# One level of Strassen's algorithm for the product of h and w2, in groups of 256 tokens

## The chip, the cores and the metric

The kernel runs on one core of a Trainium2 chip. The metric is the device time of one execution in microseconds (us). Times are medians of several executions; only executions in the fast state are compared. One slow execution occurred in the study and is named where it occurred. Engines are named as in the profile: PE is TensorE, PEld its weight loads, DVE VectorE, ACT ScalarE, POOL GpSimd. A record is one matmul in the trace; each fp32 matmul of the program leaves two. The pitch is the distance from the start of one record to the start of the next. The banks are those of PSUM, the memory into which TensorE writes; a bank is emptied (evicted) when ScalarE or VectorE has read it out. "Kernel before" and "changed kernel" are the two that the prediction compares.

## The reference

The program is an attention block with a threshold, followed by a Fourier mixing block and a channel MLP. All data are fp32.

```python
# attention: q, k, v of shape (8, 8, 576, 64)
scores = scale * np.matmul(q, k.transpose(0, 1, 3, 2))
thresh = np.max(scores, axis=-1, keepdims=True) - tau
scores = np.where(scores >= thresh, scores, -1000000000.0)
attn = softmax(scores)                       # written out in the reference
x = (attn @ v).transpose(0, 2, 1, 3).reshape(8, 576, 512)
# mixing
mixed = np.real(np.fft.fft(np.fft.fft(x, axis=1), axis=2))
u = x + mixed
un = (u - mean(u)) / np.sqrt(var(u) + 1e-06)
ch = np.maximum(un @ w_ch1, 0.0) @ w_ch2     # w_ch1 512 x 2048, w_ch2 2048 x 512
return u + ch                                # 4608 rows (tokens) of 512
```

Only the last product, `h @ w_ch2`, changes its algorithm. It has 4608 x 2048 x 512 multiplications and is one of the two largest.

## The kernel before

Eight sequences are taken in turn; each has four pairs of heads, and each pair is worked off in five steps of 128 query rows. A step computes scores, does the softmax on ScalarE and VectorE, and transposes the weights of the step before through PSUM. Between these parts `fill()` puts pieces of the mixing and of the MLP of earlier sequences into the stream of TensorE:

```python
for i in range(2 * per_batch, total + 1):
    if i < total:
        scores(i)
        softmax(i)
    fill()
    n, t = divmod(i, NT)
    transposed_weights(i - 1)      # pe, pw, pw: three PSUM banks, emptied by ScalarE
    if t == 3 and n + 1 < B * NPAIR:
        prep_pair(n + 1)           # pq, pk, pt: three more banks
    fill()
    fill()
    ...                            # weighted values, folding, start of a batch
```

The MLP works on groups of 384 tokens. `u_t` holds u transposed in a ring of two sequences. All PSUM tiles of this code except the scores share four banks (`tag="mm", bufs=4`):

```python
def channels(g):                                  # GT = 384, NJ = 16, ND = 4, DM = 512
    ...
    for j in range(NJ):                           # first product: h = relu(u w1)
        ph = ps.tile([128, 512], FP32, tag="mm", bufs=4, name="ph")
        for c in range(ND):
            nc.tensor.matmul(ph[:, 0:GT], w1[c][:, 128*j : 128*(j+1)],
                             u_t[:, c, c0 : c0 + GT], start=(c == 0), stop=(c == ND - 1))
        ...                                       # relu by ScalarE or VectorE into hT
        yield 4 * ND * GT
    for t in range(nt):                           # second product: h w2
        po = ps.tile([128, DM], FP32, tag="mm", bufs=4, name="po")
        for j in range(NJ):
            nc.tensor.matmul(po[:, :], hT[j // 4][:, j % 4, 128*t : 128*(t+1)], w2[j],
                             start=(j == 0), stop=(j == NJ - 1))
            if j % 2 == 1 and j < NJ - 1:
                yield 2 * 4 * DM
        # u += rstd * po on VectorE, then the store
```

## Time and profile before

| | before |
|---|---|
| time, median (range) | 1748.92 us (1747.66 to 1750.58), 3 runs |
| span in the profile | 1748.2 us |
| PE busy | 1704.8 us |
| VectorE, ScalarE, GpSimd busy | 867.8, 662.6, 318.7 us |
| matmul records of ph and po | 1536 and 1152 |

The lines that carry the prediction are shown in it. For the later comparison, here is the view by stretches of the kernel before: the stretch and its length, then the busy us (and number of instructions) of PE, PEld, VectorE, ScalarE and GpSimd, the granted clock of TensorE, the share of the DMA engines, and GB/s.

```profile
0.00:400.00 400.00, 367.72 (x1892) 218.74 (x1893) 276.20 (x654) 220.55 (x471) 176.81 (x259) 0.99 0.26 73
400.00:1540.00 1140.00, 1132.78 (x5268) 651.93 (x5267) 567.41 (x1423) 423.17 (x984) 133.48 (x228) 1.00 0.09 22
```

In the second stretch PE is busy 99% of the time and VectorE, ScalarE and GpSimd half of it or less. This is where a shorter stream of TensorE can shorten the kernel.

### The profile page before, as it was taken

What the parts mean: (1) busy time and instruction counts of PE and PEld (TensorE: products, weight loads), DVE (VectorE), ACT (ScalarE), POOL (GpSimd) and SP (SyncE); (2) the same over time, 40 slices, a digit from 0 to 9 for tenths busy, and PEclk for the clock granted to TensorE, in tenths of its full rate; (3) what the DMA queues carried; (4) which work ended last, traced back from release to release, by engine and by line L of the source; (5) the groups of instructions that cost most, each with busy time, mean ns of one, the idle gap of its engine ahead of it and who ended that gap; (6) DMA issues with size and microseconds to landing.
All of it is one profiled execution on the core that took longest, in us unless ns stands there. A gap on an engine that the chain in (4) does not pass through costs nothing.

```text
span 1748.2 us, 21447 instructions
## 1 busy us (share of the span) xinstructions
PE 1704.8 (98%) x7766; PEld 977.7 (56%) x7766; DVE 867.8 (50%) x2123; ACT 662.6 (38%) x1510; POOL 318.7 (18%) x499
## 2 busy tenths in 40 slices
PE   8988989999999999999999999999999999999999
PEld 4555555555565556566555556556556555555453
DVE  6886875544445555544343655644434555511010
ACT  5764764333243444334233435333324334411010
POOL 5673552020010311020110202011101031010000
PEclk9999999999999999999999999999999999999999
DMA  5313221100110111010000110101001010000000
GB/s 162 104 52 105 86 76 34 30 14 14 32 26 15 28 28 31 17 33 14 20 26 15 26 33 22 28 26 25 9 26 28 24 30 7 1 13 6 12 7 18
DMA packets 130351, 57.01 MB, mean 33 GB/s; under 512 B 121123, under 2 KB 121125, under 8 KB 130246
## 3 DMA queue, kind: packets, MB, share of 16 engines
q1 hardware_dynamic: 128854, 55.35, 11.6%
q8 instruction: 62, 1.02, 0.2%
q10 hardware_dynamic: 1392, 0.30, 0.1%
q14 instruction: 43, 0.35, 0.1%
HBM read 46.02 MB, written 9.44 MB: 32 GB/s over the span
## 4 chain that ended last, share of the span: by engine, by line
PE 84%; DVE 7%; ACT 4%; issue 3%; DMA 1%; SPq 1%; POOL 0%; ACTq 0%; DVEq 0%; POOLq 0%
PE ph L744 27%; PE po L765 27%; PE pv L551 8%; PE sc L417 7%; PE pw L530 6%; DVE e L461 2%; PE sc L428 2%; ACT e L453 1%; PE py L650 1%; DVE neg L445 1%; PE pa L667 1%; PE pa L671 1%; PE pe L513 1%; PE pn L725 1%; DVE w L290 1%
## 5 line engine op out<-in xcount | busy, mean ns | idle before, releaser
L744 PE MATMUL ph<-u_t,w 128*128 128x384 f32 x1536 | 521.7, 489 | 3.2 <-ACT e_t L532 1.1
L765 PE MATMUL po<-w,h 128*128 128x512 f32 x1152 | 524.4, 597 | 0.0
L744 PEld LDWEIGHTS ph<-u_t,w 128*128 128x128 f32 x1536 | 282.2, 190 | 189.9 <-issue 12.6
L445 DVE TENSOR_REDUCE neg<-sc 128x1 f32<-128x576 f32 x288 | 205.9, 752 | 358.7 <-PE sc L417 284.6
L453 ACT ACTIVATE e<-sc,neg 128x576 f32<-128x576 f32 x288 | 211.7, 735 | 350.4 <-DVE neg L445 349.5
L765 PEld LDWEIGHTS po<-w,h 128*128 128x128 f32 x1152 | 207.9, 190 | 221.4 <-issue 220.1
L461 DVE SCALAR_TENSOR_TENSOR e<-sc,thr,e 128x576 f32<-128x576 f32 x288 | 227.4, 814 | 81.9 <-ACT thr L457 81.1
L417 PE MATMUL sc<-kT,qT 64*128 64x288 f32 x1024 | 167.2, 431 | 7.5 <-DVE e L461 7.0
L530 PE MATMUL pw<-ident,e 128*128 128x128 f32 x1152 | 154.3, 273 | 10.7 <-ACT kT L392 4.9
L530 PEld LDWEIGHTS pw<-ident,e 128*128 128x128 f32 x1152 | 130.4, 140 | 38.1 <-issue 14.1
L750 ACT ACTIVATE h<-ph 128x384 f32<-128x384 f32 x96 | 47.1, 491 | 262.9 <-PE ph L744 262.8
L532 ACT COPY e_t<-pw 128x512 f32<-128x512 f32 x256 | 139.9, 593 | 10.6 <-PE pw L530 10.1
L417 PEld LDWEIGHTS sc<-kT,qT 64*128 64x128 f32 x1024 | 93.2, 187 | 86.7 <-issue 61.0
L582 POOL TENSOR_TENSOR half<-x 128x287 f32<-128x287 f32 x48 | 40.0, 855 | 542.1 <-ACT x L557 238.4
L689 POOL TENSOR_TENSOR u_t<-x,tmp 128x289 f32<-128x289 f32 (+1 forms) x47 | 36.4, 785 | 539.7 <-DVE tmp L686 539.4
L752 DVE TENSOR_SCALAR h<-ph 128x384 f32<-128x384 f32 x96 | 53.2, 554 | 161.8 <-PE ph L744 161.7
L477 DVE TENSOR_SCALAR e<-e,den 128x576 f32<-128x576 f32 x216 | 115.4, 572 | 3.4
L772 DVE SCALAR_TENSOR_TENSOR u<-po,rstd,u 128x512 f32<-128x512 f32 x36 | 26.9, 748 | 123.1 <-PE po L765 123.1
L557 ACT COPY x<-pv 128x288 f32<-128x288 f32 x48 | 19.2, 399 | 149.9 <-PE pv L551 133.8
L551 PE MATMUL pv<-e_t,v_rev 128*64 128x288 f32 x512 | 69.7, 415 | 3.3 <-ACT h L750 3.3
L551 PE MATMUL pv<-e_t,v_in 128*64 128x288 f32 x512 | 70.1, 417 | 0.2 <-ACT e_t L534 0.2
L520 ACT COPY ends<-pe 128x128 f32<-128x128 f32 (+1 forms) x128 | 37.2, 291 | 73.0 <-PE pe L513 62.8
(147 smaller groups left out, 1506.8 us busy)
## 6 DMA issues: line engine op xcount, KB each, us to landing
stage<-in_moe_w_ch_dram SPq DMA_DIRECT2D x26, 512.0 KB, 4.2
out_dram<-u SPq DMA_DIRECT2D x36, 256.0 KB, 2.0
qk_in<-in_q_dram SPq DMA_DIRECT2D x64, 128.0 KB, 2.3
v_in<-in_v_dram SPq DMA_DIRECT2D x64, 128.0 KB, 2.4
qk_in<-in_k_dram SPq DMA_DIRECT2D x31, 128.0 KB, 2.4
w<-in_moe_w_ch_dram SPq DMA_DIRECT2D x6, 512.0 KB, 8.4
qk_in<-in_k_dram SPq DMA_DIRECT2D x31, 64.0 KB, 2.2
qk_in<-in_k_dram SPq DMA_DIRECT2D x93, 16.0 KB, 2.1
```

Of the source, the lines that this page charges most:

```text
L417: nc.tensor.matmul(sc[j][:, c, 0:HALF], qT[hp, 128 * t : 128 * t + 128], kT[hp, HALF * c : HALF * (c + 1)], start=True, stop=True,)
L445: nc.vector.tensor_reduce(out=neg[:, j : j + 1], in_=sc[j][:, :, 0:HALF], axis=AXIS_XY, op=ALU.max, negate=True,)
L453: nc.scalar.activation(out=ej, in_=sc[j][:, :, 0:HALF], func=ACT.Exp, bias=neg[:, j : j + 1], scale=1.0)
L461: nc.vector.scalar_tensor_tensor(out=ej, in0=sc[j][:, :, 0:HALF], scalar=thr[:, j : j + 1], in1=ej, op0=ALU.is_ge, op1=ALU.mult, accum_out ...
L477: nc.vector.tensor_scalar(out=e[:, S * j : S * (j + 1)], in0=e[:, S * j : S * (j + 1)], scalar1=den[:, j : j + 1], scalar2=None, op0=ALU.mult,
L530: nc.tensor.transpose(pw[:, c, :], e[:, c0 : c0 + 128], ident[:, :])
L532: nc.scalar.copy(e_t[:, 4 * j : 4 * j + 4, qs], pw[:, :, :])
L551: nc.tensor.matmul(pv[64 * j : 64 * j + 64, 0:HALF], vt[:, 2 * c + j, :], e_t[:, 4 * j + c, cols] if c < 4 else ends[:, 0, cols], start=(c ...
L744: nc.tensor.matmul(ph[:, 0:GT], w1[c][:, 128 * j : 128 * (j + 1)], u_t[:, c, c0 : c0 + GT], start=(c == 0), stop=(c == ND - 1),)
L750: nc.scalar.activation(out=ht, in_=ph[:, 0:GT], func=ACT.Relu)
L752: nc.vector.tensor_relu(ht, ph[:, 0:GT])
L765: nc.tensor.matmul(po[:, :], hT[j // 4][:, j % 4, 128 * t : 128 * (t + 1)], w2[j], start=(j == 0), stop=(j == NJ - 1),)
```

## The change

The intent is to multiply less. From the third group on, 256 tokens and w2 are each cut into quarters, and the product of the two takes seven products of quarters in place of eight, with sums of quarters before and after. The arrangement is the one with 15 additions: with a for quarters of h and b for quarters of w2,

- sums of h: S1 = a10 + a11, S2 = S1 - a00, S3 = a00 - a10, S4 = a01 - S2 (GpSimd, 128 x 128 pieces);
- sums of w2: T1 = b01 - b00, T2 = b11 - T1, T3 = b11 - b01, T4 = T2 - b10 (VectorE, 128 x 256 pieces). There is room for one of them, so it is turned from one into the next, up and down the list in alternate groups; the negative of T4 replaces b01 for good;
- products: a00 b00, a01 b10, S2 T2, S4 b11, a11 T4, S1 T1, S3 T3, each 8 matmuls of 256 columns. Three of them (a00 b00, then + S2 T2, then - a11 T4) accumulate in one PSUM bank, `sum_`, which is read in between and so kept over the four products that follow its first.

The first two groups stay at 384 tokens. Beside this, transposes of a step are now handed out in parts between the three fillings (the **spread order**), and two tiles of the first two batches are split, which costs two small copies in place of one. All of h now lies in one tile, `hs`. In the diffs below, `...` stands for lines left out.

```diff
-    GT = 384
-    NG = B * S // GT
+    GT, BT = 384, 256
+    FIRST = 2
+    NG = FIRST + (B * S - FIRST * GT) // BT
+    NK = NJ // 2
...
+    def channels_in_quarters(g):
+        if g == FIRST:
+            first_sums()
+        up = (g - FIRST) % 2 == 0
...
+        for count in range(NJ):
+            p, k = divmod(count, 2)
+            hidden(g, count, NK * k + p, h[NK * k + p])
+            if k == 1:
+                pool.tensor_tensor(out=s_sum[p], in0=a[1][0][p], in1=a[1][1][p], op=ALU.add)
+                if not up:
+                    pool.tensor_tensor(out=s_sum[p], in0=s_sum[p], in1=a[0][0][p], op=ALU.subtract)
+                pool.tensor_tensor(
+                    out=a[1][0][p], in0=a[0][0][p], in1=a[1][0][p], op=ALU.subtract
+                )
+            yield 4 * ND * BT
...
+        def product(bank, left, right, start):
+            for p in range(NK):
+                nc.tensor.matmul(
+                    bank[:, 0 : DM // 2], left[p], right[p],
+                    start=start and p == 0, stop=p == NK - 1, skip_group_check=True,
+                )
...
+        yield from fifth() if up else seventh()
+        combine(nc.vector, t_sum, b10, minus_t4, ALU.subtract)
+        if up:
+            combine(pool, s_sum, s_sum, a[0][0], ALU.subtract)
+        sum_ = bank()
+        yield from product(sum_, a[0][0], b00, True)
+        rows.add(0, LEFT, sum_[:, 0 : DM // 2])
+        yield 4 * DM
+        yield from alone(a[0][1], b10, (0, LEFT))
+        combine(pool, a[0][1], a[0][1], s_sum, ALU.subtract)
+        yield from product(sum_, s_sum, t_sum, False)
+        rows.add(0, RIGHT, sum_[:, 0 : DM // 2])
+        rows.add(1, RIGHT, sum_[:, 0 : DM // 2])
...
+        yield from alone(a[0][1], b11, (0, RIGHT))
...
+        yield from product(sum_, a[1][1], minus_t4, False)
+        rows.add(1, LEFT, sum_[:, 0 : DM // 2])
+        yield 4 * DM
+        yield from seventh() if up else fifth()
...
+        n, t = divmod(i, NT)
+        nothing = iter(())
+        prep = prep_in_parts(n + 1) if t == 3 and n + 1 < B * NPAIR else nothing
+        weights = weights_in_parts(i - 1)
+        next(prep, None)
         fill()
-        n, t = divmod(i, NT)
-        transposed_weights(i - 1)
-        if t == 3 and n + 1 < B * NPAIR:
-            prep_pair(n + 1)
+        next(weights, None)
         fill()
+        next(weights, None)
+        next(prep, None)
         fill()
+        next(prep, None)
```

## The prediction

> **What bounds the kernel now.** I read the page first, its busy shares and the 40 slices, then the costliest groups, then the chain that ended last, then the timeline of the last 120 us, where nothing but the two products runs, and of one stage in the middle.
>
> ```profile
> PE 1704.8 (98%) x7766; PEld 977.7 (56%) x7766; DVE 867.8 (50%) x2123; ACT 662.6 (38%) x1510; POOL 318.7 (18%) x499
> PE 84%; DVE 7%; ACT 4%; issue 3%; DMA 1%; SPq 1%; POOL 0%; ACTq 0%; DVEq 0%; POOLq 0%
> L744 PE MATMUL ph<-u_t,w 128*128 128x384 f32 x1536 | 521.7, 489 | 3.2 <-ACT e_t L532 1.1
> L765 PE MATMUL po<-w,h 128*128 128x512 f32 x1152 | 524.4, 597 | 0.0
> ```
>
> TensorE (PE) is busy 98% of the span, 84% of the chain that ended last is its own, and the two products, ph (u times w1) and po (h times w2), wait for next to nothing. Busy alone would not prove much, since the ends are modelled, so I take the pitch from starts:
>
> ```profile
> 1684.89 18.23 PE L744 MATMUL ph<-u_t,w 128*128 128x384 f32 x56
> 1702.95 41.36 PE L765 MATMUL po<-w,h 128*128 128x512 f32 x96
> ...
> 1716.89 0.75 DVE L772 SCALAR_TENSOR_TENSOR u<-po,rstd,u 128x512 f32<-128x512 f32 x1 [13.18 <-PE po L765]
> ...
> 1730.62 0.75 DVE L772 SCALAR_TENSOR_TENSOR u<-po,rstd,u 128x512 f32<-128x512 f32 x1 [12.98 <-PE po L765]
> ```
>
> 56 ph records take 1702.95 - 1684.89 = 18.06 us, **322.5 ns** each; 32 po records (one bank, 16 matmuls of two records each) take 1730.62 - 1716.89 = 13.73 us, **429.1 ns** each. A line through 384 and 512 columns has 0.833 ns a column and 2.6 ns a record. The change uses 256 columns, where the weight load (190 ns in the records) might no longer hide. The mixing stage has shorter matmuls with the same full load:
>
> ```profile
> 988.12 0.41 PE L667 MATMUL pa<-seq_even,y_e 128*128 128x145 f32 x2
> ...
> 988.50 0.31 PEld L667 LDWEIGHTS pa<-seq_odd,y_e 128*128 128x128 f32 x2
> ...
> 989.11 1.88 PE L765 MATMUL po<-w,h 128*128 128x512 f32 x4
> ```
>
> From 988.12 to 989.11 run 8 such records (145 and 144 columns), 124 ns each, and the line says 123. Two loads start within 0.31 us here, so a recorded load of 190 ns overlaps its neighbour, and full loads keep up with a pitch of 124 ns. At 256 columns I therefore take 0.833 x 256 + 2.6 = **216 ns** a record, no penalty for the weight load.
>
> How full is the stream? Two batches repeat with a period of 411.5 us (the same piece of the chain begins at 951.19 and 1362.72 us). Adding pitches over that period (three groups: 384 ph records x 322.5 ns and 288 po records x 429.1 ns; then scores, transposes, weighted values and mixing at their own lengths) gives about 391 us. The other 20 us go mostly at the changes to and from the 64-row score matmuls: 8 records take 1.17 us, 0.2 us over their length, and the record before them has 0.1 us more. The change leaves these alone. So a us off the PE stream is nearly a us off the time from 400 us on.
>
> **What the Trainium skill says.** "TensorE: Matmul & The Clock Gate", section "Back-to-back issue gap", gives N/2.4 + 2.5 ns for a warm array. The trace agrees if one fp32 record is two passes (0.833 = 2/2.4, 2.6 ns fixed). The same section says that for small N in a stream of load and matmul pairs the formula under-counts; the 145-column records above do not show that. "GPSIMD Engine Reference", section "3.1 Elementwise — side-by-side cycle accounting", puts a two-input fp32 operation at about 2.6 cycles an element on GpSimd (2.2 ns at its 1.2 GHz) and about one on VectorE. The trace: GpSimd 501 ns for 143 and 855 ns for 287 elements, 2.5 ns each; VectorE 300 and 454 ns, 1.1 ns each. "SBUF — State Buffer", section "Who interferes with whom", says that a VectorE operation with two SBUF inputs and a GpSimd operation that reads SBUF exclude each other for a whole instruction. The trace before is too thin in such pairs to show it; the change makes many.
>
> **The change part by part.** Groups 0 and 1 stay at 384 tokens; 3840 tokens, ten groups before, become 15 groups of 256.
>
> *Second product.* Removed: 10 groups x 3 x 16 x 2 = 960 po records x 429.1 ns = 411.9 us. Added: 15 groups x 7 products x 8 x 2 = 1680 records x 215.8 ns = 362.5 us. **-49.4 us**, the eighth that Strassen saves less a little for shorter records.
>
> *First product.* Removed 10 x 16 x 4 x 2 = 1280 records x 322.5 = 412.8 us; added 15 x 128 = 1920 x 215.8 = 414.3 us, and in two groups whose tokens wrap round the ring each matmul is cut in two halves of 128, 0.3 us a group. **+2 us.** Transposes of u are the same in number.
>
> *Sums on GpSimd.* Groups alternate between 32 and 40 additions of 128x128: 8 x 32 + 7 x 40 = 536, each 501 - 15 x 2.5 = 464 ns, 249 us in all, so 319 becomes about 565 us, a third of the span. Beside other work.
>
> *Sums and adds on VectorE.* First weight sums 32, then 16 a group: 272 additions of 128x256, by the line through 143 and 287 elements 420 ns each, 114 us. Ten half-width adds a group: 512 columns take 748 ns, the score mask's 576 take 814, so 256 about 480; 150 x 0.48 - 30 x 0.748 = +50 us. Relus +6 us. Together about +170 us: 868 becomes about 1035 us, 60%. Beside PE as long as nothing waits.
>
> *Order.* Transposed weights and the next pair's transposes are now split and spread over the three fillings of a step. The built program shows this on PE, with the same count of score matmuls. A switch between transposes and products cost less than 0.05 us before, so more switches cost little; the split helps where fewer PSUM banks circulate.
>
> *Start.* In the first two batches one ScalarE copy of 128x256 (373 ns) becomes two of 128x128 (263 ns): +0.15 us in 32 steps and +0.3 us in 8, 7 us of ScalarE. ScalarE is about 60% busy there and the chain goes mostly through other engines: I choose +2 us. The end: two half adds of 0.48 in place of one of 0.75, +0.2 us.
>
> Sum on the path: -49.4 + 2 + 2 + 0.2 = -45 us. **For new waits I set +5 us** (a choice: a third of a us in each of 15 groups), less 2 us of old waits that the spreading takes away. 1748.9 - 42 = **1707 us**, 2.4% less.
>
> **The rivals.**
> 1. *GpSimd becomes late.* In the tail one pair of ph matmul sets takes 16 x 216 ns = 3.45 us and feeds two or three sums, 0.9 to 1.4 us, so it keeps up. For it: in the mixing stage its queue also holds 12 additions to u_t of 0.75 us, which wait for PE and VectorE, and products behind them wait for sums in the same queue. A few us in each of six batches would make 1715 to 1725.
> 2. *VectorE becomes late.* A burst of 8 weight sums is 3.4 us. The built order shows them partly threaded between softmax operations, and the softmax of a step may take until the next step, 5.7 to 10.5 us later. Against it: 40% free. If each of 30 bursts cost PE 1 us: 1735, same within 2%.
> 3. *PSUM.* One sum bank is kept over four products, beside the bank of the product in work, so two of four circulate; before, three did. In the built program at least 3 us of PE work lie between reuses where I looked. I give it 0 to 10 us.
> 4. *The weight load shows at 256 columns.* Every 10 ns a record would cost 3600 x 10 ns = 36 us and eat the gain. The 145-column records speak against it.
> 5. *Better than counted*: all sums hidden, old waits gone: 1697.
>
> **Range and chances.** The stream's -47 us is firm to about 2 us; the waits are one-sided, 0 to 20 us. So 1697 to 1726 holds it 8 times in 10. The line of 2% is near 1714.5, 7 us above my figure: faster 0.74, within 2% 0.25, slower 0.01.
>
> **What would show it.** po records 1872 (192 + 1680) and ph records near 2430 (256 + 2176), both of 256 columns at a pitch of 216 ns; busy PE about 45 us less; GpSimd near 565 us and VectorE near 1035; idle time of po charged to GpSimd or VectorE under 10 us. I am wrong if the pitch at 256 columns is above 220 ns, if PE shows tens of us of waits on sums, on additions to u_t or on evictions, or if the first 400 us grow by over 5 us.

## The result, and the profile after

The changed kernel took **1707.53 us** (median of 4 runs, 1705.46 to 1711.78) against 1749.54 us for the kernel before in the same rounds. All four executions of the changed kernel were in the fast state. The ratio is 0.9764 with a 95% interval of 0.9743 to 0.9785. A ratio here is the mean time of one kernel's fast runs over the mean of the other's fast runs of the same rounds, so it is not quite the ratio of the medians.

The page of the changed kernel: busy us, share of the span and number of instructions; the chain that ended last by engine; and two groups (line, engine, operation, tiles, shapes, count, then busy us, mean ns and idle time before them).

```profile
PE 1658.9 (97%) x9382; PEld 1241.3 (73%) x9382; DVE 1047.2 (61%) x2560; ACT 685.6 (40%) x1609; POOL 583.4 (34%) x1035
...
PE 88%; ACT 5%; DVE 4%; DMA 1%; SPq 1%; issue 1%; POOL 0%; ACTq 0%; DVEq 0%; POOLq 0%
...
L805 PE MATMUL ph<-u_t,w 128*128 128x256 f32 (+2 forms) x2432 | 538.6, 371 | 5.6 <-ACT y_e L684 4.1
...
L898 PE MATMUL po<-w,hs 128*128 128x256 f32 x960 | 228.0, 382 | 0.0
```

PE is busy 45.9 us less and the span is 42.0 us shorter (1748.2 - 1706.2). The po groups together have 1680 records of 256 columns and the 192 of the first two groups; ph has 2432. None of po's records waits to speak of. One new wait shows in ph's line, 4.1 us for a ScalarE copy to y_e.

The timeline of PE in the last products (start us, length, instruction, count) gives the pitch:

```profile
1677.87 3.62 PE L898 MATMUL po<-hs,s_tile 128*128 128x256 f32 x16
1681.33 7.07 PE L898 MATMUL po<-w,hs 128*128 128x256 f32 x32
1688.23 3.62 PE L898 MATMUL po<-hs,s_tile 128*128 128x256 f32 x16
```

48 records take 1688.23 - 1677.87 = 10.36 us, 215.8 ns each, as worked out in the prediction. Seven products follow each other without a gap.

The groups of VectorE and GpSimd by form show what the sums cost:

```profile
L856 DVE TENSOR_TENSOR hs<-w,w 128x256 f32<-128x256 f32 x120 | 58.1, 520 | 6.3 <-PE po L898 6.3
...
L856 DVE TENSOR_TENSOR hs<-w,hs 128x256 f32<-128x256 f32 x72 | 44.1, 653 | 0.6 <-PE po L898 0.4
...
L856 DVE TENSOR_TENSOR hs<-hs,w 128x256 f32<-128x256 f32 x64 | 27.4, 453 | 2.2 <-PE po L898 2.1
...
L883 POOL TENSOR_TENSOR s_tile<-hs 128x128 f32<-128x128 f32 x120 | 58.5, 487 | 572.0 <-DVE hs L812 463.1
```

They are longer than the prediction's 420 and 464 ns, and it did not matter: the engines had room. In the same two stretches as before:

```profile
0.00:400.00 400.00, 367.02 (x1902) 218.56 (x1902) 279.57 (x658) 227.38 (x525) 176.25 (x259) 0.99 0.26 74
400.00:1540.00 1140.00, 1129.69 (x6720) 880.19 (x6719) 714.17 (x1782) 443.84 (x1034) 356.57 (x672) 1.00 0.09 22
```

**Where the time went.** To split the gain I gave every matmul record its ideal length (0.833 ns for each column plus 2.45 ns, from the pitches above; half the column part for a record that uses half the array's rows or columns, since two of those run side by side: the 64-column pv records of 288 columns follow each other at 122.6 ns on average). The distance from its start to the next record's start, less this length, is the excess: waits, changes between kinds of matmul, and time at a lower granted clock. The sums, in us:

| kernel | ideal stream | excess |
|---|---|---|
| before | 1597.1 | 145.1 |
| after | 1550.2 | 150.0 |
| difference | -46.9 | +4.9 |

The ideal stream is itself counts times pitch, so its difference checks the counts and no more; that the pitch holds is shown by the tail above, and the rest is the excess. The stream shrank by what the counts say, and a net 5 us of waits came back. What lies behind the net 5 us is what the experiments are about.

### The profile page after: what moved, and what is told of

The parts are those of the page before. It is cut to its first block, busy times and chain, and to the rows that moved or that the text cites. A ratio compares the mean times of both kernels' runs of the same rounds, so it can differ in the third digit from the quotient of the medians.

```text
span 1706.2 us, 26144 instructions
## 1 busy us (share of the span) xinstructions
PE 1658.9 (97%) x9382; PEld 1241.3 (73%) x9382; DVE 1047.2 (61%) x2560; ACT 685.6 (40%) x1609; POOL 583.4 (34%) x1035
## 4 chain that ended last, share of the span: by engine, by line
PE 88%; ACT 5%; DVE 4%; DMA 1%; SPq 1%; issue 1%; POOL 0%; ACTq 0%; DVEq 0%; POOLq 0%
PE ph L805 29%; PE po L898 22%; PE pv L575 9%; PE sc L431 8%; PE pw L554 6%; PE po L828 5%; PE sc L442 2%; ACT e L467 2%; DVE e L475 1%; PE py L674 1%; PE pa L691 1%; PE pa L695 1%; DVE neg L459 1%; PE pe L535 1%; PE pn L765 1%; PE pq L396 1%
## 5 line engine op out<-in xcount | busy, mean ns | idle before, releaser
L805 PE MATMUL ph<-u_t,w 128*128 128x256 f32 (+2 forms) x2432 | 538.6, 371 | 5.6 <-ACT y_e L684 4.1
L805 PEld LDWEIGHTS ph<-u_t,w 128*128 128x128 f32 x2432 | 412.1, 190 | 84.8 <-issue 10.1
L883 POOL TENSOR_TENSOR s_tile<-hs 128x128 f32<-128x128 f32 x120 | 58.5, 487 | 572.0 <-DVE hs L812 463.1
L898 PE MATMUL po<-w,hs 128*128 128x256 f32 x960 | 228.0, 382 | 0.0
L898 PEld LDWEIGHTS po<-w,hs 128*128 128x128 f32 x960 | 175.5, 190 | 27.7 <-issue 6.2
L812 DVE TENSOR_SCALAR hs<-ph 128x256 f32<-128x256 f32 (+1 forms) x136 | 59.3, 436 | 141.1 <-PE ph L805 130.4
L787 DVE SCALAR_TENSOR_TENSOR u<-po,rstd,u 128x256 f32<-128x256 f32 (+1 forms) x156 | 72.9, 486 | 84.2 <-PE po L898 82.1
L898 PE MATMUL po<-hs,s_tile 128*128 128x256 f32 x480 | 113.9, 382 | 0.0
L898 PEld LDWEIGHTS po<-hs,s_tile 128*128 128x128 f32 x480 | 88.4, 190 | 14.2 <-issue 2.9
L828 PE MATMUL po<-w,hs 128*128 128x512 f32 x192 | 89.9, 599 | 0.0
```

Of the source, the lines that this page charges most:

```text
L787: nc.vector.scalar_tensor_tensor(out=u, in0=product, scalar=self.rstd[:, t : t + 1], in1=u, op0=ALU.mult, op1=ALU.add,)
L805: nc.tensor.matmul(ph[:, a:z], w1[c][:, 128 * j : 128 * (j + 1)], u_t[:, c, at : at + z - a], start=(c == 0), stop=(c == ND - 1), skip_gro ...
L828: nc.tensor.matmul(po[:, :], h[j][:, 128 * t : 128 * (t + 1)], w2[j], start=(j == 0), stop=(j == NJ - 1),)
L898: nc.tensor.matmul(bank[:, 0 : DM // 2], left[p], right[p], start=start and p == 0, stop=p == NK - 1, skip_group_check=True,)
```

## The experiments

There were twelve runs, each with five rounds against the kernel before. The kernel before had medians between 1749.86 and 1750.38 us in them. Where two kernels come from different calls, I compare their ratios to the kernel before.

| label | what it is | median us (range) | ratio to before [95%] |
|---|---|---|---|
| after_again | the change, as it is | 1708.19 (1707.99 to 1708.84) | 0.9762 [0.9749, 0.9775] |
| order_only | all groups 384, plain, spread order | 1743.16 (1742.22 to 1746.79), four fast runs | 0.9965 [0.9951, 0.9979] |
| plain256 | groups of 256, plain, spread order | 1741.49 (1740.31 to 1744.38) | 0.9952 [0.9939, 0.9966] |
| plain256_old | groups of 256, plain, old order | 1754.13 (1752.58 to 1755.68) | 1.0022 [1.0011, 1.0033] |
| old_order | Strassen, old order | 1725.15 (1723.69 to 1726.64) | 0.9858 [0.9845, 0.9872] |
| unkept | Strassen, no kept bank | **1701.52** (1700.02 to 1703.84) | 0.9722 [0.9708, 0.9735] |
| old_unkept | Strassen, no kept bank, old order | 1717.25 (1714.39 to 1721.87) | 0.9811 [0.9795, 0.9827] |
| no_sums | Strassen without sums (wrong on purpose) | 1706.79 (1705.58 to 1709.77) | 0.9757 [0.9743, 0.977] |
| pool_twice | each GpSimd sum done twice | 1720.24 (1718.2 to 1722.09) | 0.983 [0.9816, 0.9843] |
| sums_vector | GpSimd's sums on VectorE | 1717.24 (1714.98 to 1718.11) | 0.9811 [0.9798, 0.9824] |
| halves | before, po in halves of 256 columns | 1753.25 (1750.64 to 1753.88) | 1.0012 [1.0005, 1.0018] |
| first0 | Strassen from the first group on | 1750.08 (1748.66 to 1751.45) | 0.9999 [0.9991, 1.0007] |

All but no_sums gave the right result.

### after_again

No edit: a control, so that the other kernels have the change beside them.

> The changed kernel unaltered, as the control of this chip: 1705 to 1710 us, ratio to before 0.976 within 0.002.

Measured: 1708.19 us, the ratio within 0.0002 of the first result. The excess in its trace is 150.2 us, against 150.0.

### order_only: the spread order without Strassen

```diff
-    FIRST = 2
+    FIRST = 12
```

Twelve groups of 384 cover all tokens, so the second product is the plain one everywhere. What is left of the change is the spread order, the split copies and the one tile for h.

> All 12 groups of 384 tokens with the plain product, but the transposes spread over the step and the copies split as in the changed kernel. Theory: copies +2, order -2, so 1749 us (1745 to 1752). Rival (the spread order is worth something by itself): below 1743 us.

Measured: 1743.16 us as the median of the four fast runs (1743.87 us with the slow one), between the theory's 1745 to 1752 us and the rival's figure of less than 1743 us. One execution, the profiled one, fell in the slow state (1965.35 us at a clock of 0.851), so its trace is not used. The spread order, with the copies that come with it, takes 0.35% or 6 us off (95%: 4 to 9 us). The prediction had -2 for old waits and +2 for the copies, that is nothing.

### plain256: smaller groups without Strassen

```diff
-        second = NJ * DM * n // 128 if g < FIRST else 7 * NK * DM // 2 * n // 256
+        second = NJ * DM * n // 128
...
-        h = [hs[:, GT * j : GT * (j + 1)] for j in range(NJ)]
+        n = tokens_of(g)[1]
+        h = [hs[:, n * j : n * (j + 1)] for j in range(NJ)]
...
-            work.append((b, channels(groups) if groups < FIRST else channels_in_quarters(groups)))
+            work.append((b, channels(groups)))
```

> Groups of 256 tokens from the third on, the spread order and the split copies kept, but h times w2 as before, 16 matmuls of 512 columns a tile, no sums. Theory (the whole gain is Strassen's eighth of h times w2): first product +2 us, copies +2, order -2, so 1751 us (1747 to 1755), about 44 us above the changed kernel. Rival (the smaller groups and the spread order carry part of the gain): 1740 us or less.

Measured: 1741.49 us. The theory (1747 us or more) fell; the rival's 1740 us was missed by 1.5 us. Its ideal stream is 1599.4 us, 2.3 more than before, as the prediction had for the first product (+2), and its excess is 137.1 us, 8.0 less than before. So the stream of the changed kernel is 49.2 us shorter than this one's, and its excess is 12.9 us longer. **Strassen itself costs 13 us of waits**; the spread order had first paid 8 of them. The traced execution of plain256 was the slowest of its five (1744.38 us), so that both numbers are some 3 us too small: by the medians they are 16 us (1741.49 - 1708.19 = 33.3 us gained, where the stream is 49.2 us shorter) and 11 us.

9.3 of the 13 us stand in the list of PE's waits. In the changed kernel (us in total, times, longest):

```profile
PE ph L805 <- ACT y_e L684: 4.1, 4, 1.0
...
PE pa L691 <- ACT e_t L558: 2.7, 4, 0.7
PE pw L554 <- ACT ends L546: 2.5, 4, 0.6
```

In plain256 none of the three is there. All stand in the mixing stages, and each occurs four times. The largest, in the timeline of PE of the changed kernel:

```profile
529.39 0.94 PE L674 MATMUL py<-dim_c,f 128*128 128x65 f32 x6
530.17 0.27 PE L535 MATMUL pe<-ident,e 128*128 128x128 f32 x1
530.28 0.60 PE L554 MATMUL pw<-ident,e 128*128 128x128 f32 x4
530.71 0.61 PE L674 MATMUL py<-dim_s,f 128*128 128x128 f32 x4
532.34 1.99 PE L805 MATMUL ph<-u_t,w 128*128 128x256 f32 x8 [1.02 <-ACT y_e L684]
```

Four banks (py, pe, pw, py) are taken within 2 us, and ph needs a fifth: it waits until the first py is empty. ScalarE empties it late; its timeline:

```profile
530.93 0.60 ACT L679 COPY y_e<-py 128x256 f32<-128x256 f32 x1
...
531.49 0.74 ACT L467 ACTIVATE e<-sc,neg 128x576 f32<-128x576 f32 x1
532.12 0.17 ACT L684 COPY y_e<-py 128x1 f32<-128x1 f32 x1
```

The last column of py is copied only after an exponential of the softmax, and 0.05 us after that ph starts. In plain256 at the same place a piece of po, 1.7 us long, stands between py and pe, and ScalarE has done the copies by the time the bank is needed. In the changed kernel that filling holds no piece of a product. So this wait comes from how the pieces fell among the transposes. It doesn't come from a sum: in no_sums, below, it is as long.

### plain256_old: the same with the old order

```diff
-        nothing = iter(())
-        prep = prep_in_parts(n + 1) if t == 3 and n + 1 < B * NPAIR else nothing
-        weights = weights_in_parts(i - 1)
-        next(prep, None)
         fill()
-        next(weights, None)
+        transposed_weights(i - 1)
+        if t == 3 and n + 1 < B * NPAIR:
+            prep_pair(n + 1)
         fill()
-        next(weights, None)
-        next(prep, None)
         fill()
-        next(prep, None)
```

This run was made last, to test a theory that the next three left.

> Groups of 256 tokens with the plain product, and the transposes of a step in one piece as in the kernel before. Theory (the worth of the spread order grows with the PSUM evictions among which the transposes must find room: per 768 tokens 38 in the kernel before, 54 here, 69 with Strassen, where the spread order was worth 17 us, and about 6 us in groups of 384): about 12 us over the spread order of the same kernel (1741.5), so 1751 to 1757 us. Rival (only Strassen's products make it worth more): about 6 us over, so 1746 to 1750 us.

Measured: 1754.13 us, within the range of the theory, outside the rival's. It is 12.6 us over plain256 by the medians and 12 us by the ratios (the two ran in different calls, on different chips). The spread order is worth 6 us in groups of 384 (against the whole kernel before), 12 us in plain groups of 256, and 16 to 17 us with Strassen, each to about 3 us.

### old_order: Strassen without the spread order

The edit is the one of plain256_old, made in the changed kernel.

> The changed kernel with the transposes of a step in one piece again, as in the kernel before. Theory (switches and old waits are small): 1707 to 1713 us. Rival (with a kept sum bank and a product's bank only two of four PSUM banks circulate, and the spreading is what makes Strassen pay): 1722 us or more.

Measured: 1725.15 us, 17 us over the control: the theory (1713 us or less) fell, and the rival's figure came true. Its reason, the kept bank, is tested by old_unkept below. The excess is 167.6 us, 17.6 more. A stretch of its timeline of PE, in a mixing stage:

```profile
541.48 1.22 PE L554 MATMUL pw<-ident,e 128*128 128x128 f32 x8
542.88 0.66 PE L396 MATMUL pq<-ident,qk_in 128*128 128x128 f32 x4 [0.18 <-ACT ends L542]
543.37 0.64 PE L403 MATMUL pk<-ident,qk_in 128*128 128x128 f32 x4
543.85 0.32 PE L407 MATMUL pt<-ident,qk_in 128*128 128x128 f32 x1
544.69 0.94 PE L674 MATMUL py<-dim_c,f 128*128 128x65 f32 x6 [0.52 <-ACT kT L404]
```

In one piece, the transposes ask for six banks in a row, and py behind them for a seventh; pq and py wait until ScalarE has emptied earlier ones. In the spread order a piece of a product lies between the transposes.

### unkept: no kept bank

```diff
-        sum_ = bank()
-        yield from product(sum_, a[0][0], b00, True)
-        rows.add(0, LEFT, sum_[:, 0 : DM // 2])
-        yield 4 * DM
+        yield from alone(a[0][0], b00, (0, LEFT), (0, RIGHT), (1, RIGHT), (1, LEFT))
...
-        yield from product(sum_, s_sum, t_sum, False)
-        rows.add(0, RIGHT, sum_[:, 0 : DM // 2])
-        rows.add(1, RIGHT, sum_[:, 0 : DM // 2])
-        yield 4 * DM
+        yield from alone(s_sum, t_sum, (0, RIGHT), (1, RIGHT), (1, LEFT))
...
-        yield from product(sum_, a[1][1], minus_t4, False)
-        rows.add(1, LEFT, sum_[:, 0 : DM // 2])
-        yield 4 * DM
+        yield from alone(a[1][1], minus_t4, (1, LEFT))
```

Every product gets its own bank and is added to all quarters of u that need it. VectorE does 14 half adds a group in place of 10, and all four banks circulate.

> The changed kernel with every product in a bank of its own, evicted at once: the first product is added to four quarters, the one that ran on in its bank to three, so 14 half adds a group in place of 10, 60 x 0.48 = 29 us more on VectorE, no bank kept over four products. Theory (of the 13 us by which waits grow between the plain groups of 256 and the changed kernel, most come from the kept bank, in the mixing stages): 1697 to 1703 us. Rival (the waits in the mixing stages are of ScalarE evictions and come back whatever is kept): 1706 to 1712 us.

Measured: 1701.52 us, ratio 0.9722 against 0.9762; the intervals do not overlap. It beats both kernels. VectorE is busy 25.8 us more (1073.0 us), the ideal stream is the same, and the excess is 142.9 us, 7.1 less. Its list of PE's waits:

```profile
PE ph L805 <- ACT y_e L684: 4.1, 4, 1.0
...
PE pa L691 <- ACT ends L546: 0.7, 4, 0.2
```

Of the three waits shown above, pw for ends (2.5 us) and pa for e_t (2.7 us) are gone, and 0.7 us stands in their place; the wait for y_e is as it was. The first two go with the kept bank: in the changed kernel they stand where a group is in its second product. The third stands in a first product, where no bank is kept. So the time is the one that the theory gave, but "most" of the 13 us (16 by the medians) was about half, and the wait for y_e came back as the rival said. Of the 7.1 us less excess, 4.5 are in these three waits; for the rest the trace names no wait.

### old_unkept: no kept bank, old order

The edits of unkept and of old_order together. If the spread order pays because one bank is kept, it should pay less here.

> The same with the step's transposes in one piece again. Theory (the spread order pays because of the kept bank): the 17 us that the old order costs with a kept bank shrink to about 8, the worth of the spread order with plain products, so 1706 to 1712 us. Rival (bank or no bank, the old order costs 17 us under Strassen): 1717 us or more.

Measured: 1717.25 us, 15.7 us over unkept, as the rival had it. With the kept bank the order was worth 17.0 us. So the theory that the kept bank makes the order pay fell; the difference of about a us is within the noise. What fits the pairs so far (three, by then) is the number of evictions of product banks for 768 tokens: 38 in the kernel before (32 of ph and 6 of po), 54 in plain groups of 256, 69 with Strassen (48 and 21). The reading is that the more often the product banks turn over, the more transposes in one piece run into banks that are not yet empty. (The 69 is exact for the kernels without a kept bank. With one, a group takes five banks for its seven products, so 63 are given back, and the order was worth no less there.) The plain256_old run, the fourth pair, was the test of this that could have failed. It remains a fit of few points; I have not varied the number of evictions alone, and the size of the pieces between the transposes changed with it.

### no_sums: the sums taken away

The result is wrong on purpose (relative error 18.2): the sums are not computed, the tiles for them are set to a constant (the one for h once a group).

```diff
     def combine(eng, out_, in0, in1, op):
-        for p in range(NK):
-            eng.tensor_tensor(out=out_[p], in0=in0[p], in1=in1[p], op=op)
+        return
...
             if k == 1:
-                pool.tensor_tensor(out=s_sum[p], in0=a[1][0][p], in1=a[1][1][p], op=ALU.add)
...
+                pass
```

> All 536 GpSimd sums and all 272 VectorE weight sums taken away (8 VectorE fills once and one GpSimd fill a group in their place), so the result is wrong on purpose; products, adds and order kept. Theory (the sums run beside PE; waits on them are at most 5 us): 1701 to 1707 us. Rival (PE waits on sums): 1697 us or less.

Measured: 1706.79 us, ratio 0.9757 against 0.9762. GpSimd lost 250 us of work and VectorE 123 us, and the time fell by a us, within the noise and within the theory's range. The excess is 148.4 us, 1.6 under the changed kernel's. **The sums are hidden.** PE's list of waits still has the largest new one, as long as with the sums:

```profile
PE ph L805 <- ACT y_e L684: 4.1, 4, 1.0
```

### pool_twice: how much room GpSimd has

Each sum on GpSimd is followed by one of the same size into a tile that is no longer used (the sums in the first product likewise, left out below).

```diff
             eng.tensor_tensor(out=out_[p], in0=in0[p], in1=in1[p], op=op)
+            if eng is nc.gpsimd:
+                eng.tensor_tensor(out=spare[:, :], in0=in0[p], in1=in1[p], op=op)
...
```

> Each GpSimd sum followed by an equal one into a tile nobody reads: GpSimd goes from 583 to about 840 us, half the span. Theory (GpSimd has room): 1706 to 1711 us. Rival (its queue is already near late, above all in the mixing stage): 1717 us or more.

Measured: 1720.24 us, 12 us over the control; GpSimd is busy 827.9 us, 48% of the span. The theory (1711 us or less) fell. The rival's figure came true, but not in the mixing stages where it looked first: of the 10.2 us more excess, 9.6 us come after 1540 us, where mostly products run, and 1.5 us between 400 and 1540 us (the start has 0.9 us less). PE in that tail:

```profile
1593.05 0.70 PE L906 MATMUL po<-w,hs 128*128 128x256 f32 x2 [0.43 <-POOL hs L857]
1594.00 0.70 PE L906 MATMUL po<-w,hs 128*128 128x256 f32 x2 [0.25 <-POOL hs L857]
1594.95 0.70 PE L906 MATMUL po<-w,hs 128*128 128x256 f32 x2 [0.25 <-POOL hs L857]
```

The two records of a quarter piece start every 0.95 us, which is two sums of GpSimd, in place of 0.43 us. A single sum takes about 0.48 us, a little more than the 0.43 us that PE needs for what it feeds. So the sums of the changed kernel stay hidden because they start a product ahead (in the code, S4 is formed while S2 T2 runs), and not because GpSimd would be faster; their busy share of 34% hides how close it is there.

### sums_vector: all sums on VectorE

```diff
-        pool = nc.gpsimd
+        pool = nc.vector
```

> The GpSimd sums moved to VectorE: 536 x 0.28 = 150 us more there, less some 40 us that its own sums now take over the 420 ns worked out (520 to 653 ns measured), so about 1155 us, 68%. Theory (all sums are beside PE): within 5 us of the changed kernel, 1703 to 1712 us. Rival (VectorE's queue carries the softmax and gets late): 1717 us or more.

Measured: 1717.24 us, 9 us over the control, with VectorE at 67%. The theory (1712 us or less) fell, the rival's figure came true. The groups of VectorE:

```profile
L856 DVE TENSOR_TENSOR hs<-w,w 128x256 f32<-128x256 f32 x120 | 46.1, 416 | 3.3 <-PE po L898 3.2
...
L856 DVE TENSOR_TENSOR hs<-w,hs 128x256 f32<-128x256 f32 x72 | 30.8, 458 | 0.1
L856 DVE TENSOR_TENSOR hs<-hs,w 128x256 f32<-128x256 f32 x64 | 25.3, 428 | 2.0 <-PE po L898 1.9
```

With GpSimd's sums gone, the same weight sums take 416, 458 and 428 ns in place of 520, 653 and 453. The 536 moved sums are shorter here too (295 to 368 ns in place of about 487). The changed kernel's own trace shows the same inside one execution: its 129 of these 256 sums during which GpSimd ran nothing took 394 to 427 ns, and the 127 others 668 ns on average (counted from the records, by whether a GpSimd record overlaps). The kernel is slower all the same, because VectorE is where the softmax runs. The wait for y_e grows from 4.1 to 8.5 us:

```profile
PE ph L805 <- ACT y_e L684: 8.5, 4, 2.2
```

In this trace four sums stand ahead of a step's row maxima in VectorE's queue, the exponentials follow the maxima on ScalarE, and the copy that frees the bank follows the exponentials.

### halves: does a weight load show at 256 columns

The kernel before, with each po matmul as two of 256 columns:

```diff
-                nc.tensor.matmul(
-                    po[:, :], hT[j // 4][:, j % 4, 128 * t : 128 * (t + 1)], w2[j],
-                    start=(j == 0), stop=(j == NJ - 1),
-                )
+                for c in (0, 256):
+                    nc.tensor.matmul(
+                        po[:, c : c + 256], hT[j // 4][:, j % 4, 128 * t : 128 * (t + 1)],
+                        w2[j][:, c : c + 256],
+                        start=(j == 0 and c == 0), stop=(j == NJ - 1), skip_group_check=True,
+                    )
```

> The kernel before with each 512-column matmul of h times w2 as two of 256 columns with the same weights: 2304 records in place of 1152. Theory (weight loads hide at 256 columns, 216 ns a record): 2304 x 215.8 - 494.3 us = +3 us, 1752 us. Rival (weight loads show): 10 ns a record would be +26 us, 1772 us or more.

Measured: 1753.25 us, ratio 1.0012, about 2 us more for 1152 more records and as many more weight loads, near the theory's 3 us and far from the rival's 26. VectorE's adds at the end mark the pitch:

```profile
1720.46 0.75 DVE L774 SCALAR_TENSOR_TENSOR u<-po,rstd,u 128x512 f32<-128x512 f32 x1 [13.26 <-PE po L766]
1734.27 0.75 DVE L774 SCALAR_TENSOR_TENSOR u<-po,rstd,u 128x512 f32<-128x512 f32 x1 [13.06 <-PE po L766]
```

64 records take 13.81 us, 215.8 ns each. The load is hidden at this size.

### first0: Strassen from the first group on

```diff
-    FIRST = 2
+    FIRST = 0
...
-                recs = sb.tile([128, S], FP32, tag="sums", bufs=1, name="recs")
+                recs = sb.tile([128, S], FP32, tag="recs", bufs=1, name="recs")
...
+        if g == FIRST:
+            while not ready:           # set once w2 has arrived
+                yield -1
+            first_sums()
```

One buffer less for rows of u pays for the extra tile (`bufs=2` in place of 3), so more than one thing differs.

> All 18 groups of 256 tokens and by Strassen, none of 384; the weight sums wait until the last of w2 has come, the split copy of the reciprocals has a room of its own, and u has two buffers in place of three. Theory (the gain is in the PE stream and so in proportion: 3840 tokens gave 46.9 us, 768 more give 9.4): 1698 to 1703 us. Rival (in the first 400 us PE isn't what sets the time, and the waiting weights push work out): 1706 us or more.

Measured: 1750.08 us, as the kernel before. The theory (1703 us or less) fell. The ideal stream fell by another 9.6 us and the excess rose by 51.5, of which 27.7 us are in the first 400 us. The first sums now stand where TensorE needs them at once: PE's wait list and timeline have

```profile
PE po L896 <- DVE hs L856: 13.5, 1, 13.5
```

one wait of 13.5 us for the 32 first sums of w2, about their length at 420 ns. In the changed kernel these sums are done during groups 0 and 1 and nothing waits for them. The granted clock fell too. This is the stretch from 200 to 300 us in first0, and then in the changed kernel, 0.83 against 0.98 (the third number from the right):

```profile
200.00:300.00 100.00, 72.57 (x369) 52.67 (x366) 78.18 (x182) 49.75 (x107) 56.39 (x74) 0.83 0.20 56
200.00:300.00 100.00, 91.55 (x476) 55.60 (x477) 74.29 (x174) 65.13 (x153) 52.84 (x68) 0.98 0.25 67
```

Over the whole span it was 0.979 to 0.982 in all 13 executions of first0 and 0.995 to 0.999 in the changed kernel's, though all count as fast; so part of the excess is not waiting but a slower array. The first records after the long wait show it:

```profile
278.67 6.19 PE L896 MATMUL po<-hs,s_tile 128*128 128x256 f32 x16 [13.50 <-DVE hs L856]
```

Sixteen records take 6.19 us here, and 3.62 us in the changed kernel; the second to the tenth of them start 426 to 427 ns apart, twice the usual pitch. In all first0 has 42 records of this size at that doubled pitch and the changed kernel none, which is about 9 us (42 x 211 ns). Among PE's waits, those of the scores for VectorE's e grew from 7.0 to 13.5 us, and waits of pw for additions to u (6.6 us) and of ph for additions to u_t (6.5 us) are new. How the loss divides between these, the clock, the smaller buffers and the group that is held back until w2 is there, I did not take apart.

## Why the prediction was right, point by point

- **Second and first product, -49.4 and +2 us.** Right. The counts are as built (1680 and 192 records of po, 2432 of ph, where the text had "near 2430"), the pitch at 256 columns is 215.8 ns, and the ideal stream is 46.9 us shorter. plain256 shows the first product alone at +2.3 us. One reading on the way was too strong: that the 20 us of a period outside the stream go "mostly" at the changes to and from the score matmuls. By the excess defined above such changes carry 12.4 of 25.0 us in that period, about half; 5.6 us stand at other changes, among them the transposes and py, which the change does move.
- **Sums on GpSimd and VectorE beside other work.** Right, shown by no_sums. The sizes were low: GpSimd 583.4 us for 565, VectorE 1047.2 for 1035. (Of the former, 3 us are a slip of addition: 319 + 249 is 568.) The prediction named the shared access to SBUF and said that the trace before was too thin to show it; it then used the durations without it. sums_vector shows the effect: 416 to 458 ns without, 453 to 653 ns with GpSimd's sums beside. The 420 ns were right for a sum with GpSimd idle (394 to 427 ns in the changed kernel); about half of them met GpSimd at work.
- **Old waits taken away by the spread order, -2 us, and its cost at the start, +2 us.** Mis-sized. Together they measured -6 us in groups of 384 (order_only), and -8.0 us of excess in groups of 256 (plain256; -11 by the medians). The copies are not seen: the excess of the first 400 us is 73.9 us before and 74.9 after.
- **New waits, +5 us.** Mis-sized the other way: 12.9 us over plain256 (16 by the medians). The 5 us were called a choice; the 9.3 us of them that the trace names are on PSUM banks in the mixing stages, not on sums.
- **The sum, -42 us.** The two mis-sized terms, some 8 us each by the excess (11 by the medians), cancelled. That is luck: the total was hit more closely (1707 for 1707.53) than its terms deserve.
- **Rivals.** The first (GpSimd late) and the second (VectorE late) did not occur; pool_twice and sums_vector show that the room for them is not large: doubling the sums on GpSimd costs 12 us, moving them to VectorE 9 us. The third (PSUM) did: the kept bank costs 7 us by unkept, within the 0 to 10 us given, and the place named for it, circulating banks, was the right one. The fourth (weight load) is refuted by halves. The fifth (1697 us) was not reached even by unkept, which has 4.1 us of the y_e wait left.
- **What was to make it wrong.** None came: the pitch is under 220 ns, and the first 400 us grew by 1 us of excess. The prediction did not name the ordering on ScalarE behind the largest new wait.

Open are why excess in the mixing stages differs by the further few us that no wait of the profile carries, and what of first0's loss belongs to which of its edits.

## What to carry to other kernels

When PE is the bound, count records times pitch first: that part of this prediction was good to half a us, while the waits were out by 8 us or more in each direction. An algorithm that trades matmuls for more and shorter products also turns PSUM banks over more often, so look next at which engine empties them and what stands ahead of it in that engine's queue; here adding the first product to four quarters, on a VectorE that was busy 61% of the span, was cheaper than keeping one bank of four. Before believing a total that came out right, run the parts of the change one at a time.

## What the Trainium skill lacked or had wrong

- "SBUF — State Buffer", section "Who interferes with whom": agrees in kind. It has no size for a mixture of short operations; here VectorE's two-input sums of 128x256 took 520, 653 and 453 ns on average with GpSimd's sums in the program and 416, 458 and 428 ns without. In one and the same trace they took 394 to 427 ns where no GpSimd record overlapped and 668 ns on average where one did.
- "TensorE: Matmul & The Clock Gate", section "Back-to-back issue gap": its formula is of one pass, N/2.4 + 2.5 ns; an fp32 record of 256 columns took 215.8 ns, which is two such passes' columns and one fixed part, and the section does not say how to apply it to fp32. It says that in a stream of loads and matmuls the formula under-counts at small N (81 ns measured at 128 columns) and over-counts at large N (131 ns at 512). With a new weight load for each record, neither shows here: 145 columns took 124 ns for the 123 of the formula with two passes, and 512 columns 429.1 ns, far above 131 for each pass. But a record that is two passes gives its load twice the time, so the first is no test of the 81 ns.
- The same page, section "LDWEIGHTS (loading the stationary operand)", gives P / 1.2 ns, 107 ns for 128 columns; the records of these products' fp32 loads have 190 ns. They hide under a pitch of 124 ns as well as of 215.8 ns, so the recorded length is not what a load adds.
- No page puts a number on what one PSUM bank fewer in rotation costs. Here one bank of four that is kept over four products cost 7 us of 1708, and handing out a step's transposes in one piece (up to six banks in a row) cost 6 to 17 us; that this grows with how often the banks of the products are emptied is a fit of four pairs, not shown by itself.
